# The first unit's V loads, SyncE transfers and hand-written order in a block-sparse attention and feed-forward kernel

## The chip, the cores and the metric

The kernel runs on one core of one Trainium2 chip. The metric is the device time of one execution in microseconds (us). Engines are named as in the profile: PE (TensorE matmuls), PEld (its weight loads), DVE (VectorE), ACT (ScalarE), POOL (GpSimd) and SP (SyncE, which here only issues transfers). Work between engines is ordered by semaphores; each engine runs its own instructions in the order in which the program wrote them.

## The reference

Four batches, eight heads, 768 tokens in 24 blocks of 32, head size 64. Every block of queries sees its own block, the two beside it, the first and the last block, and three sampled blocks; the first and last query block see everything ("dense" rows). The attention output then goes through a feed-forward layer with exact GELU (512 to 2048 to 512).

```
scores = q @ k.T / sqrt(64)                    # per batch and head
mask   = |blk_i - blk_j| <= 1 or blk_i, blk_j in {0, 23} or blk_j in sampled_blocks[blk_i]
attn   = softmax(where(mask, scores, -1e9))
x      = (attn @ v)  as (3072, 512)
out    = gelu_exact(x @ w_in) @ w_out
```

## The kernel before

The work is cut into eight units, two for each batch. Unit 0 of a batch has the query blocks 1 to 11 in three groups of four, four and three (groups 0, 1, 2 of the plan: blocks 4-7, 8-11, 1-3) and the dense rows; unit 1 has blocks 12 to 22. A unit's attention is followed by its feed-forward layer: first `ffn1` products (`hp`, L540), GELU, then `ffn2` products (`op`, L583), which are strewn as fillers into the attention of the next unit. `ffn1` of unit 0 is begun ahead in the attention of unit 0 (`ffn1_ahead`).

The scores of a group of query blocks need, for each block, its keys side by side in the tile `gb`: the first and last block ("fixed", copied by `gather_fixed` with part 1), the three neighbours (part 0), and the three sampled blocks, which `gather` copies one by one, with block numbers held in registers (`block_numbers` loads them from the list `vf`, at line L231, in one register load for up to 22 numbers). In the first unit POOL gathers the sampled keys of groups 1 and 2 (`gather(..., 0, KC, nc.gpsimd)`, 128 columns) and later the sampled values of all three groups (`values_of(t)`, 264 columns, into the tiles `kn` and `g`, which are free then). DVE gathers the sampled keys of group 0. SP copies the fixed blocks of groups 1 and 2: `fixed(1, nc.sync, 1)` gives four transfers, `fixed(2, nc.sync, 1)` two.

V of a batch is loaded by POOL in eight transfers, one for each head, in the order `VORDER` (`load_values`, L149), into `kvs[b % 2]`. Before the lines below, three of the eight have been issued, behind two loads of k (`kn`) and two of q (`qn`):

```
others = block_numbers(grps[1], POOL)      # L674
load_values(0, slice(3, 7))
others |= block_numbers(grps[2], POOL)
load_values(0, slice(7, None))
```

After them POOL gathers the keys of group 1 (6, then 6, with `load_w_in(0)` between), loads the numbers of group 0, issues `load_w_in(1)` and gathers the 9 blocks of keys of group 2. Then `xv0`, `xv1`, `xv2` gather the values of groups 0, 1, 2, with `load_w_in(2)`, `load_w_in(3)` and both halves of `w_out` strewn in, and `xl` loads k and q of batch 1.

The order of everything else in a unit's attention is a plan written out by hand, a string of words. `s0` to `s3` are scores of the four dense rounds, `s4`/`s5`, `s6`/`s7`, `s8`/`s9` of the rounds of groups 0, 1, 2 (two query blocks each, one in s9). `m` is the maximum (DVE), `e` the exponentials (ACT), `t` the turning of the exponentials (DVE). `w` is the product with values for the dense rows (`wd`, in halves `wd0`, `wd1`) or a group (`wa`, `wb`, `wc`: L484), `d` the division (DVE), `o`/`O` the turning of the output (PE, then copied by ACT). `f` with a number issues that many filler products (in unit 0: `idle_products`, L593, whose results nobody uses), 32 in all. `x` with a name calls one of the extra steps: `xp2`, `xp3` turn the q heads of pairs 2 and 3; `xf0`, `xf1`, `xf2` are ACT's copies of neighbours for groups 1 and 2; `xh`, `xi`, `xj` are DVE's for group 0; `xa`, `xb`, `xc` are `ffn1` products ahead; `xn` loads numbers on DVE; `G` loads ACT's table for GELU. Scores go to one of two buffers (`psA`), so that a round of scores waits until the exponentials two rounds earlier are done.

In unit 1, `PLANS[1]` (`xk0d` and so on) turns k and q of batch 1 on PE, at L242, from the tiles that `xl` loads.

Of the kernel before, what the change touches and what calls it, by code (L numbers as in the profile page):

```python
# [11 lines left out]
BF16 = mybir.dt.bfloat16  # L12
# [8 lines left out]
def kernel(  # L21
# [10 lines left out]
    nc = tc.nc  # L32
    P = 128
    B, H, S, D = q.shape
# [9 lines left out]
    VS = 2 * D + 4  # L44
    KC = NPR * BL
# [13 lines left out]
    const = ctx.enter_context(tc.tile_pool(name="const", bufs=1))  # L59
# [11 lines left out]
    kvs = [const.tile([P, NB + 1, BW], BF16, name=f"kv{i}") for i in range(2)]  # L71
# [10 lines left out]
    g = const.tile([P, KOUT, UT], BF16, name="g")  # L82
    mark = const.tile([1, 1], BF16, name="mark")
    junk = const.tile([1, 1], BF16, name="junk")

    HALVES = (slice(0, 4), slice(4, 8))

# [57 lines left out]
    def load_v(b, h):  # L145
        G, hh = divmod(h, 4)
        c0 = KC + VS * G + D * (hh % 2)
        hh ^= G
        nc.gpsimd.dma_start(out=kvs[b % 2][32 * hh:32 * hh + 32, 0:NB, c0:c0 + D],  # L149
                            in_=v[b, h].rearrange("(n p) d -> p n d", p=BL))  # L150


    VORDER = sorted(range(H), key=lambda h: (h // 4, (h % 4 ^ h // 4) % 2, h % 4))

    def load_values(b, at=slice(None)):
        for h in VORDER[at]:
            load_v(b, h)
# [17 lines left out]
    def ones(i):  # L175
        for hh in range(4):
            for G in range(2):
# [6 lines left out]
                      in_=bass.AP(tensor=sb_words, offset=0,  # L184
                                  ap=[[NB * NR * 2, 1], [1, NB * NR * 2]]))
# [40 lines left out]
    def block_numbers(js, engine):  # L226
        flat = vf.rearrange("o j r -> o (j r)")
        vals = []
        for c0 in range(js[0] * NR, (js[-1] + 1) * NR, 22):
            c1 = min(c0 + 22, (js[-1] + 1) * NR)  # L230
            _, got = nc.values_load_multi_w_load_instructions(  # L231
                flat[0:1, c0:c1], engines=[engine], min_val=0, max_val=NB,
                skip_runtime_bounds_check_because="block numbers are below the number of blocks")
            vals += got if isinstance(got, (tuple, list)) else [got]
        return {j: vals[NR * i:NR * i + NR] for i, j in enumerate(js)}
# [46 lines left out]
    def gather_fixed(kT, place, copy=None, part=None, lanes=range(3)):  # L282

        copy = copy or nc.vector.tensor_copy
        groups = gb.rearrange("p (g x) -> p g x", x=GW)
        js = sorted(place)
        runs = [[j for j in js if place[j] - j == c] for c in sorted({place[j] - j for j in js})]
        for run in runs if part != 1 else ():
            i0 = place[run[0]]
            assert i0 % 3 == 0  # L290
            for lane in range(min(3, len(run))):
                if lane not in lanes:
                    continue
                m, g0 = len(range(lane, len(run), 3)), i0 // 3
                c0, j = BW + KC * lane, run[0] + lane - 1
                copy(
                    groups[:, g0:g0 + m, c0:c0 + 3 * BW].rearrange("p g (w c) -> p g w c", c=BW)[:, :, :, 0:KC],
                    kT[:, j:j + 3 * m, :].rearrange("p (g w) c -> p g w c", w=3))
        if part == 0:
            return  # L300
        at = slice(min(place.values()) // 3, max(place.values()) // 3 + 1)
        n = at.stop - at.start
        for to, n0 in ((groups[:, at, 0:3 * KC].rearrange("p g (l c) -> p g l c", c=KC), 0),
                       (groups[:, at, 4 * BW:GW].rearrange("p g (l x) -> p g l x", x=DW)[:, :, :, NR * BW:DW], NB - 1)):
            if copy is nc.sync:
                for x in range(n):
                    nc.sync.dma_start(out=to[:, x], in_=kT[:, n0:n0 + 1, :].to_broadcast([P, 3, KC]))
            else:
                copy(to, kT[:, None, n0:n0 + 1, :].to_broadcast([P, n, 3, KC]))

    def gather(unit, js, at, c0=0, c1=BW, engine=None):

        src = k0 if (unit.b, c1) == (0, KC) else kvs[unit.b % 2][:, :, c0:c1]
        for j in js:
            for r in range(NR):
                to = sampled_values(unit, j, r) if c0 == KC else sampled(unit.place[j], r)[:, c0:c1]
                (engine or nc.vector).tensor_copy(to[:, None, :], src[:, bass.ds(at[j][r], 1), :])  # L317
# [271 lines left out]
    def idle_products(m):  # L589

        op = psO.tile([P, D_MODEL], F32, name="op", tag="op")
        for _ in range(m):
            nc.tensor.matmul(op, lhsT=identity, rhs=qT0[:, 0:2, 0:2, :], start=True, stop=True)  # L593
            yield
# [77 lines left out]
    grps = units[0].groups  # L672
    value_list()
    others = block_numbers(grps[1], POOL)  # L674
    load_values(0, slice(3, 7))
    others |= block_numbers(grps[2], POOL)
    load_values(0, slice(7, None))
    known = block_numbers(grps[0], DVE)
    nc.vector.memset(kvs[1][:, FILLED:NB + 1, KC:BW], 0.0)
    known |= block_numbers(J0[7:9], DVE)  # L680
# [14 lines left out]
    def fixed(t, *how):  # L695
        gather_fixed(k0, {j: units[0].place[j] for j in grps[t]}, *how)
    fixed(1, nc.sync, 1)
    fixed(2, nc.sync, 1)
    gather(units[0], grps[1][:2], others, 0, KC, nc.gpsimd)
    load_w_in(0)  # L700
# [24 lines left out]
    def more_numbers(js):  # L725
        def load():
            for c in range(0, len(js), 6):
                known.update(block_numbers(js[c:c + 6], DVE))
        return load
    attention(units[0], idle_products(32),  # L730
# [3 lines left out]
              {"l": later_keys, "p2": partial(later_pair, 0), "p3": partial(later_pair, 1),  # L734
               "h": lambda: fixed(0, None, 0, (0,)), "i": lambda: fixed(0, None, 0, (1, 2)),
               "j": lambda: fixed(0, None, 1),
# [29 lines left out]
    for n, unit in enumerate(units):  # L766
# [3 lines left out]
        if nxt is not None and not fresh:  # L770
            if n == 0:
                nc.vector.tensor_copy(kvs[0][:, :, 0:KC], k0)
                more_numbers(J1[3:8])()
            gather_fixed(keys(b), nxt.place)
            gather(nxt, J1[:8], known)
            if n == 0:
                more_numbers(J0[:3])()
        for s in range(KOUT // 2):
            ffn1_step(n, 2 * s)
            if s == 0:  # L780
# [4 lines left out]
                elif fresh and b + 2 < B:  # L785
                    xT, t0 = column[b, unit.groups[-2][0]]
# [17 lines left out]
            if fresh and s == 0:  # L804
                gather_fixed(keys(b + 1), nxt.place)
                gather(nxt, J0[3:9], known)
                gather(nxt, J0[:3], known)
                hold_loads(sampled(nxt.place[J0[2]], NR - 1)[0:1, BW - 1:BW])
                gather(nxt, J0[9:], others, engine=nc.gpsimd)
# [43 lines left out]
```

## Time and profile before

| | us |
|---|---|
| median of 3 runs | 274.44 (274.05 to 274.59) |
| profiled execution, its own time | 273.89 |
| its span, first to last instruction | 271.9 |
| PE busy in the span | 255.1 (94%) |
| DVE busy | 203.2 (75%) |
| ACT busy | 207.0 (76%) |
| POOL busy | 103.0 (38%) |

Rows of the timeline give start, duration, engine, line, operation, output tile <- input tiles, how many instructions the row holds, and in brackets the engine's idle time before them and what ended it. "issue" there means that the profile shows nothing that the engine waited for. Rows of the chain give start, duration and what the chain was on. Rows of one line's view give the durations (ns, least/median/most) and the first and last start. Rows of the windows give the stretch, its length, the busy time of PE, PEld, DVE, ACT and POOL with the number of instructions, the granted PE clock, the share of the transfer engines and GB/s.

### The profile page before, as it was taken

The numbers are of one execution on the slowest core, as the hardware profiler recorded it, in microseconds if no ns is written. First come the engines' busy times: TensorE is split into PE (matmuls) and PEld (weight loads), VectorE is DVE, ScalarE is ACT, GpSimd is POOL, SyncE is SP. The second block draws the span as 40 slices with busy tenths as digits, with TensorE's granted clock in tenths as the row PEclk, the third lists the DMA queues.
The fourth block names the chain that finished last, engine by engine and source line by source line (L and its number), as shares of the span: only waits on it lengthen the run. The fifth ranks groups of instructions, "written<-read, shape, count | busy, mean of one in ns | idle before, by whom it ended". The sixth has DMA issues, their size and how long they took to land.

```text
span 271.9 us, 11545 instructions
## 1 busy us (share of the span) xinstructions
PE 255.1 (94%) x4944; PEld 144.8 (53%) x4944; DVE 203.2 (75%) x472; ACT 207.0 (76%) x379; POOL 103.0 (38%) x212
## 2 busy tenths in 40 slices
PE   0789699999999999999999999999999999999995
PEld 0634485455664665545554466455645655465544
DVE  7599758699896989589998987698939993882000
ACT  8789746977868886797868976988788966995611
POOL 7798960735964000950963002920040160000000
PEclk9999979999999999999999999999999999999999
DMA  6999399979999115951999108911101110111012
GB/s 98 185 185 144 66 140 201 206 129 146 95 172 129 41 43 122 122 65 50 104 164 123 60 28 159 112 43 45 40 0 41 46 41 0 41 41 43 0 40 78
DMA packets 75909, 24.40 MB, mean 90 GB/s; under 512 B 65489, under 2 KB 72914, under 8 KB 75858
## 3 DMA queue, kind: packets, MB, share of 16 engines
q0 software_dynamic: 57440, 13.64, 53.7%
q1 hardware_dynamic: 18418, 10.03, 15.5%
q8 instruction: 38, 0.62, 1.0%
q14 instruction: 13, 0.11, 0.1%
HBM read 27.26 MB, written 6.29 MB: 123 GB/s over the span
## 4 chain that ended last, share of the span: by engine, by line
PE 71%; DMA 9%; ACT 7%; POOL 6%; issue 4%; DVE 2%; POOLq 1%; ACTq 0%
PE hp L540 27%; PE op L583 21%; PE av L484 9%; DMA kn<-in_k_dram 6%; PE sc L358 4%; DMA kv<-in_v_dram 3%; ACT L429 2%; PE tx L516 2%; PE op L612 2%; PE av L445 2%; POOL g L317 2%; ACT pp L401 2%; PE pt L242 1%; POOL kv L149 1%; PE av L612 1%
## 5 line engine op out<-in xcount | busy, mean ns | idle before, releaser
L540 PE MATMUL hp<-xT,w_in_sb 128*128 128x384 bf16 (+2 forms) x536 | 85.1, 319 | 0.2 <-issue 0.2
L583 PE MATMUL op<-w_out_sb,g 128*128 128x512 bf16 x336 | 83.9, 380 | 0.4 <-issue 0.4
L401 ACT ACTIVATE pp<-sc,nm 128x256 bf16<-128x256 f32 x176 | 74.4, 546 | 7.5 <-DVE nm L384 7.5
L540 PEld LDWEIGHTS <-w_in_sb 128*128 128x128 bf16 x536 | 51.2, 98 | 33.3 <-issue 0.3
L562 ACT ACTIVATE g<-hp 128x768 bf16<-128x768 f32 x56 | 45.2, 809 | 25.4 <-PE hp L540 25.4
L384 DVE TENSOR_REDUCE nm<-sc 128x4 f32<-128x1024 f32 (+1 forms) x48 | 53.2, 1117 | 10.5 <-PE sc L358 10.2
L583 PEld LDWEIGHTS <-g 128*128 128x128 bf16 x336 | 28.6, 98 | 34.3 <-issue 7.2
L317 DVE COPY gb<-kv 128x392 bf16 x177 | 34.7, 274 | 0.0
L418 DVE STREAM_TRANSPOSE pT<-pp 128x512 f32<-128x512 f32 (+1 forms) x48 | 31.2, 657 | 4.3 <-ACT pp L401 3.8
L317 POOL COPY gb<-kv 128x392 bf16 x54 | 26.3, 537 | 16.1 <-PE av L484 15.7
L173 POOL COPY mark<-gb 1x1 bf16<-1x1 bf16 x6 | 1.1, 178 | 81.3 <-DVE gb L317 81.3
L484 PE MATMUL av<-kv,pT 64*32 64x130 bf16 (+1 forms) x1344 | 28.7, 228 | 1.0 <-DVE pT L418 0.9
L484 PEld LDWEIGHTS <-pT 64*32 64x32 bf16 (+1 forms) x2400 | 26.8, 94 | 5.1 <-DVE pT L418 2.6
L149 POOL DMA_DIRECT2D kv<-in_v_dram x32 | 22.9, 726 | 2.4 <-issue 2.3
L524 ACT COPY xT<-tx 128x512 bf16<-128x512 bf16 (+1 forms) x32 | 13.9, 459 | 11.6 <-PE tx L516 11.3
L358 PE MATMUL sc<-gb,qT 64*32 64x256 bf16 x704 | 18.4, 274 | 2.9 <-issue 1.5
L358 PEld LDWEIGHTS <-qT 64*32 64x32 bf16 x832 | 9.5, 89 | 21.2 <-issue 13.4
L429 ACT ACT_TABLE_LOAD x15 | 19.2, 1283 | 0.2
L387 DVE TENSOR_REDUCE nm<-sc 128x1 f32<-128x768 f32 x16 | 14.7, 947 | 5.9 <-PE sc L358 5.7
L504 DVE TENSOR_TENSOR xh<-av,rec 128x512 bf16<-128x512 f32 (+2 forms) x28 | 18.3, 652 | 1.0
L567 ACT COPY os<-op 128x512 f32<-128x512 f32 (+1 forms) x23 | 13.1, 570 | 6.0 <-PE op L612 4.3
L484 PE MATMUL av<-gb,pT 64*32 64x130 bf16 x924 | 17.2, 222 | 0.0
(80 smaller groups left out, 249.6 us busy)
## 6 DMA issues: line engine op xcount, KB each, us to landing
out_dram<-os SPq DMA_DIRECT2D x23, 256.0 KB, 2.4
kv<-in_v_dram POOLq DMA_DIRECT2D x32, 96.0 KB, 3.7
w_in_sb<-in_moe_w_in_dram POOLq DMA_DIRECT2D x4, 512.0 KB, 7.3
w_out_sb<-in_moe_w_out_dram POOLq DMA_DIRECT2D x2, 1024.0 KB, 13.4
kn<-in_k_dram POOLq DMA_DIRECT2D x4, 384.0 KB, 11.4
qn<-in_q_dram POOLq DMA_DIRECT2D x4, 384.0 KB, 12.8
qn<-in_q_dram POOLq DMA_DIRECT2D x12, 128.0 KB, 4.9
kn<-in_k_dram POOLq DMA_DIRECT2D x12, 128.0 KB, 6.0
```

What stands on the lines that cost most here:

```text
L149: nc.gpsimd.dma_start(out=kvs[b % 2][32 * hh:32 * hh + 32, 0:NB, c0:c0 + D], in_=v[b, h].rearrange("(n p) d -> p n d", p=BL))
L317: (engine or nc.vector).tensor_copy(to[:, None, :], src[:, bass.ds(at[j][r], 1), :])
L358: nc.tensor.matmul(o, lhsT=qT[rows, j // 4, pr, BL * (j % 4):BL * (j % 4) + BL], rhs=rhs(rows, pr), start=True, stop=True)
L384: nc.vector.tensor_reduce(out=nm[:, 0:2 * n].rearrange("p (g j) -> p g j", g=2), in_=A4[:, :, 0:n, :], op=ALU.max, axis=AX.X, negate=True)
L401: nc.scalar.activation(at[:, x // n, x % n], A[:, a:a + 256].rearrange("p (e c k) -> p e c k", e=2, k=BL), AF.Exp, bias=nm[:, x:x + 1])
L418: nc.vector.transpose(pt.rearrange("p g c x -> p (g c) x")[:, :, 64 * s:64 * (s + n)].bitcast(F32), pp[:, 0:512 * n].bitcast(F32).rearrang ...
L429: nc.scalar.activation(junk, zero[0:1, 0:1], func)
L484: nc.tensor.matmul(av[32 * s:32 * (s + w), h, VS * G:VS * G + V2], lhsT=pv[rows, G, c % 4, BL * s:BL * (s + w), c // 4], rhs=src[rows], st ...
L504: nc.vector.tensor_tensor(xh[rows, :, 0:m * D].rearrange("p h (g x d) -> p h g x d", x=2, d=D), a[:, :, :, 0:2 * D].rearrange("p h g (x d) ...
L540: nc.tensor.matmul(hp[:, i, c0:c1], lhsT=w_in_sb[:, ki, (m + i) * P:(m + i + 1) * P], rhs=xTs[n % 2][:, ki, c0:c1], start=(ki == 0), stop= ...
L562: nc.scalar.activation(g[:, m:m + 2, 0:T], hp[:, :, 0:T], AF.Gelu)
L583: nc.tensor.matmul(op, lhsT=g[:, m, t * P:(t + 1) * P], rhs=w_out_sb[:, m, :], start=(m == 0), stop=(m == KOUT - 1))
```

## The change

The eighth V load is issued with the fourth to seventh, ahead of the register load of group 2's block numbers. On SP a small transfer of two elements of the last V head into a new tile `seen` is placed between the four transfers of group 1 and the two of group 2; it reads what the last V load writes, so SP waits there until that load has landed, and group 2's transfers come behind it. The plan of unit 0 is another order of the same words: 32 filler products as before, 23 instead of 28 of them ahead of `s9`; `xf0` and `xh` stand first, `s5` and `m5` ahead of `t3` and `t2`, `xf2` behind `e5`, `G` behind `wb`. In `gather_fixed` the source is named once; the copies are the same.

```
+    seen = const.tile([1, 2], BF16, name="seen")
...
-    load_values(0, slice(3, 7))
+    load_values(0, slice(3, None))
     others |= block_numbers(grps[2], POOL)
-    load_values(0, slice(7, None))
     known = block_numbers(grps[0], DVE)
...
     fixed(1, nc.sync, 1)
+
+    hh, c0 = VORDER[-1] % 4 ^ VORDER[-1] // 4, KC + VS * (VORDER[-1] // 4) + D * (VORDER[-1] % 2)
+    nc.sync.dma_start(out=seen, in_=kvs[0][32 * hh:32 * hh + 1, 0, c0:c0 + 2])
     fixed(2, nc.sync, 1)
...
-              "xj xp2 xv0 s0 xp3 s1 m0 f1 xv1 f1 e0 xi m1 e1 xh s2 f1 s3 t0 xf0 m2 e2 f1 m3 t1 e3 f2 s4 xf1 f8 m4 "
-              "e4 t3 t2 s5 f1 xf2 wd0 s6 f1 xv2 wd1 f2 m5 f2 e5 t4 m6 f2 dd s7 t5 e6 m7 od f2 s8 t6 wa xl e7 f4 "
-              "m8 s9 da e8 m9 t7 t8 e9 t9 f2 oa wb wc db ob dc xn xa Oc xb f2 G xc",
+              "xf0 xj xh xp2 s0 xp3 m0 xv0 s1 f1 e0 xi s2 m1 e1 f1 s3 f1 t0 f1 m2 e2 m3 t1 e3 f3 s4 xv1 f1 m4 s5 "
+              "m5 t3 f1 xf1 t2 f3 xv2 e4 e5 f3 s6 wd0 wd1 f2 t4 xf2 m6 s7 dd t5 e6 f3 m7 e7 f2 s8 od t6 wa xl m8 "
+              "e8 da f1 s9 m9 t7 f4 e9 t8 t9 f3 oa wb G db wc ob dc xn f1 xa Oc xb f1 xc",
```

More of the change, by code (lines that the diff above doesn't have):

```diff
@@ L304, in gather_fixed @@
                        (groups[:, at, 4 * BW:GW].rearrange("p g (l x) -> p g l x", x=DW)[:, :, :, NR * BW:DW], NB - 1)):
+            fixed_block = kT[:, None, n0:n0 + 1, :].to_broadcast([P, n, 3, KC])
             if copy is nc.sync:
                 for x in range(n):
-                    nc.sync.dma_start(out=to[:, x], in_=kT[:, n0:n0 + 1, :].to_broadcast([P, 3, KC]))
+                    nc.sync.dma_start(out=to[:, x], in_=fixed_block[:, x])
             else:
-                copy(to, kT[:, None, n0:n0 + 1, :].to_broadcast([P, n, 3, KC]))
+                copy(to, fixed_block)
     def gather(unit, js, at, c0=0, c1=BW, engine=None):
```

## The prediction

> **What bounds the kernel now.** I read the page first, then the chain that ended last in order of time, then the timeline of each engine over the first 55 us, since the change touches nothing later.
>
> ```profile
> span 271.9 us, 11545 instructions
> PE 255.1 (94%) x4944; PEld 144.8 (53%) x4944; DVE 203.2 (75%) x472; ACT 207.0 (76%) x379; POOL 103.0 (38%) x212
> ```
>
> TensorE (PE) is busy for 94% of the span, so time is lost or won only where PE waits. The chain shows where the first unit is tied to something else than PE:
>
> ```profile
> 10.82 0.71 POOLq L231
> 11.53 1.44 issue
> 12.99 7.93 DMA kv<-in_v_dram
> ...
> 33.55 0.69 POOL w_in_sb L162
> 34.24 1.73 POOL w_out_sb L167 x2
> 35.97 16.87 DMA kn<-in_k_dram
> ```
>
> The reader is to see that for the first 53 us the chain is not on PE. It goes through GpSimd (POOL): reading block numbers, the eighth V load, that load's flight, a row of gathers, three weight loads, the load of batch 1's keys (kn). Those keys land at 35.97 + 16.87 = 52.84 and PE turns them at 52.88. How far PE is from being the bound itself at that point:
>
> ```profile
> 52.88 0.53 PE L242 MATMUL pt<-identity,kn 96*64 96x96 bf16 x16 [0.47 <-DMA kn<-in_k_dram]
> ```
>
> PE waits 0.47 us for kn. So two paths meet at 52.88: the POOL path, and PE's own work, which is 0.47 us shorter. From there PE runs on almost without a gap. Whichever path is later after the change sets the new time. A gain of PE alone in the first unit is worth nothing, and a gain of POOL alone at most 0.47 us; a loss of POOL counts in full.
>
> **The POOL path, step by step.**
>
> ```profile
> 8.70 2.83 POOL L149 DMA_DIRECT2D kv<-in_v_dram  x4 [0.25 <-issue]
> 12.99 0.71 POOL L149 DMA_DIRECT2D kv<-in_v_dram  x1 [1.46 <-issue]
> 13.75 1.47 POOL L317 COPY gb<-qT 128x128 bf16 x6
> ...
> 18.24 2.17 POOL L317 COPY gb<-qT 128x128 bf16 x9
> 21.24 3.20 POOL L317 COPY kn<-kv 128x264 bf16 x9 [0.84 <-DMA kv<-in_v_dram]
> ...
> 26.16 7.38 POOL L317 COPY g<-kv 128x264 bf16 x21
> 33.50 0.74 POOL L162 DMA_DIRECT2D w_in_sb<-in_moe_w_in_dram  x1
> 34.23 1.77 POOL L167 DMA_DIRECT2D w_out_sb<-in_moe_w_out_dram  x2
> 35.97 0.71 POOL L118 DMA_DIRECT2D kn<-in_k_dram  x1
> ```
>
> Seven V loads are out by 11.53. Then come the third group's nine block numbers, the eighth V load at 12.99, and the key gathers, which run without a gap from 13.75 to 18.24 + 2.17 = 20.41. POOL then stands 0.84 us until V has landed (12.99 + 7.93 = 20.92; the first value gather is at 21.24). From 21.24 to the issue of kn at 35.97 it has no hole: every shift at 21.24 reaches kn. So the most that an earlier V can give here is the hole of 0.84 us, and only if the key gathers don't move.
>
> They do move. The change puts the eighth V load ahead of the nine numbers, and both are in POOL's instruction order ahead of the first key gather. What the numbers cost, from the rows of the register loads (by the code: nine values from element 3 of the list in the first row, twelve from 24, twelve from 12, nine from 60, and on VectorE (DVE) fifteen from 45 and nine from 3):
>
> ```profile
> L231 POOLq TENSOR_LOAD <-vf x1: 2273/2273/2273, 10.2 to 10.2; - x1
> L231 POOLq TENSOR_LOAD <-vf x1: 1025/1025/1025, 7.1 to 7.1; - x1
> L231 POOLq TENSOR_LOAD <-vf x1: 1236/1236/1236, 15.0 to 15.0; - x1
> L231 POOLq TENSOR_LOAD <-vf x1: 827/827/827, 32.4 to 32.4; - x1
> L231 DVEq TENSOR_LOAD <-vf x1: 3410/3410/3410, 38.1 to 38.1; - x1
> L231 DVEq TENSOR_LOAD <-vf x1: 2061/2061/2061, 47.5 to 47.5; - x1
> ```
>
> The lists that begin at an element divisible by 4 cost 0.83 to 1.24 us, the others (3, 45, 3) 0.23 to 0.25 us a value. The third group begins at 3, so it costs 2.27 us and not about 1. In the kernel before, this read begins at 10.2 while POOL is still busy issuing V loads six and seven: of its 2.27 us, 1.3 lie beside that work. After the change it can begin only when the eighth V load has been handed out, and that load has a wait of its own: the view of the second q load lists it among those that waited for its landing (the load that comes eight places earlier in POOL's row of loads). The first row below is that entry, the others show when PE saw the two q loads.
>
> ```profile
>   POOL kv L149: 1.5, 1
> 9.95 0.85 PE L242 MATMUL pq<-identity,qn 96*64 96x96 bf16 x16 [0.37 <-DMA qn<-in_q_dram]
> 12.02 0.85 PE L242 MATMUL pt<-identity,qn 96*64 96x96 bf16 x16 [0.57 <-DMA qn<-in_q_dram]
> ```
>
> The first q load has landed just before 9.95 and the second just before 12.02. The seventh V load waits in the same way for the first, and the register load behind it began at 10.2: 0.2 to 0.3 us after that landing. So I put the eighth V load at 12.0 (1.0 us earlier than now), and the register load at 12.2, done at 12.2 + 2.27 = 14.5. Now: done at 12.44, and the next instruction on the engine at 12.99, which is 0.55 us for moving the numbers; with 0.15 us for the gather's own address the first key gather comes 0.7 us behind, at 15.2 instead of 13.75: 1.4 us later. The key gathers then end at 20.41 + 1.4 = 21.8. V is down by then: it was down at 20.92, is issued 1.0 us earlier, and two SyncE transfers no longer run beside it. The 0.84 us hole is gone, and the value gathers begin at 21.8 instead of 21.24: 0.6 us later. What was hidden (1.3 us of register load beside V loads) now stands open, and it is more than the hole that it closes.
>
> Bounds of this term: a register load of 0.83 us, the cheapest row, would start the key gathers at 12.2 + 0.83 + 0.7 = 13.7, as now; V, some 0.5 us earlier at 20.4, plus the 0.3 us that the first gather took behind the landing, starts the value gathers at 20.7: -0.5 us. A register load of 2.5 us gives +0.85. I take +0.6, since the same nine numbers from the same place cost 2.27 and 2.06.
>
> [...]
>
> The kn load then goes out at 36.6 and, the queue ahead of it (the same three weight loads) being shifted with it, lands at 53.4; PE turns it at 53.5: +0.6 us.
>
> **SyncE's transfers.** Before, six of them are issued from 10.55 on; four remain, and the last two follow a two-element read that waits for V.
>
> ```profile
> 10.55 6.00 SPq L307 DMA_DIRECT2D gb<-qT  x6
> DMA to landing us min/median/max: 7.3/7.6/9.6
> ```
>
> Nothing else stands in SyncE's queue until the first output. The two are issued at about 20.8 and 21.5. In the crowd of V loads such a transfer took 7.3 to 9.6 us; here only weight loads run beside it, so I take about 4 to 5 us, landing at 25 to 26.5, with 31.1 as the far end. Who waits: the scores of the third group (s8, s9).
>
> ```profile
> 27.08 0.41 PE L358 MATMUL sc<-gb,qT 64*32 64x256 bf16 x16 [0.35 <-ACT pp L401]
> ...
> 31.33 0.29 PE L358 MATMUL sc<-gb,qT 64*32 64x256 bf16 x4 [1.47 <-issue]
> 31.56 0.60 PE L593 MATMUL op<-qT,identity 128*128 128x512 bf16 x2
> ```
>
> s8 is at 27.08 and, by the new order, again near 27 (it still needs the exponentials two rounds back). Cost taken: nothing, with up to 4 us at the far end.
>
> **The new order.** ScalarE's (ACT's) window copies xf0 move ahead of the turned q heads into idle time; xf2 moves behind e5, which lets e5 run earlier; DVE does m5 before t3 and t2, so the dense values wd start about 1 us later, while the second half of wd now follows the first directly. I estimate these to cancel by s8. After s9, seven filler products instead of two stand before the second group's values (wb), and the table load G moves to where ACT is idle; ACT is not what PE waits for there. PE's clock:
>
> ```profile
> 29.95:33.36 3.41, 1.37 (x18) 0.74 (x17) 1.88 (x4) 1.86 (x6) 3.41 (x11) 1.00 0.02 5
> 33.36:36.78 3.42, 3.42 (x195) 3.21 (x192) 1.73 (x6) 0.47 (x2) 3.42 (x6) 0.50 0.53 55
> ```
>
> PE was busy for 1.37 of 3.41 us, and in the next 3.42 us its granted clock (the third figure from the end) was 0.50. More fillers before wb may keep the clock up, worth 3.42 x 0.5, at most 1.7 us; or they only push wb back by five products (0.60 / 2 each: at most 1.5 us). PE thus comes to kn between 1.7 us earlier and 1.5 us later. It may be 0.47 + 0.6 = 1.1 us later before it costs anything. I take zero: kn covers the whole reordering, either way.
>
> The sum: 0 (PE side, covered) + 0.6 (kn later) = +0.6 us on the profiled execution's 273.89, which lies 0.55 below the median of the runs, 274.44. On the median: 275.0, +0.2%.
>
> **Rivals.**
> *The register load is no hindrance* (the other sign): it costs about 1 us behind the V load, or runs ahead of the wait, the key gathers stay at 13.75, and V's earlier landing counts. For it: three of four POOL loads cost 0.83 to 1.24. Against it: the start at element 3. The price is worked out above: value gathers at 20.7, kn 0.5 us earlier, 273.9 if PE keeps up, 274.4 if PE is half a microsecond later itself. It decides where the first key gather starts at 14.3 or earlier (then key gathers end before 21.0 and POOL gains).
> *PE becomes the late path*: SyncE's two transfers land after 27.5 and hold s8, and with it od, wa and s9 in PE's order; or PE, now waiting over 1 us for kn, has its clock halved once more (up to 1.7 us). For it: the 7.3 to 9.6 us row. Against it: 1.1 us of cover. It gives +0.9 to +2 us: 275.3 to 276.4. [...]
> *The change moves V no earlier*: the landing may be set by the packets in flight, not by the issue at 12.99. By the forecast that does not matter, because the key gathers end later than V lands; it stays +0.6.
>
> **How the numbers follow.** Forecast (with the third rival, same time): 0.53. Register load no hindrance: 0.25. PE late: 0.22. A measurement of this kernel can tell about 0.2% (0.55 us) from no change. The forecast's own spread, +0.4 to +0.85, straddles that: 0.27 of its 0.53 count as slower, 0.26 as same. Of the second case, 0.12 faster and 0.13 same; all of the third is slower. Together 0.12 faster, 0.39 same, 0.49 slower. The range is 274.0 to 276.3: it takes in most of the cases on both sides and leaves out the ends of the second (below 274.0) and of the third (above 276.3). The likeliest case's own range is 274.8 to 275.3.
>
> **What would show it.** Right: the eighth V load near 12.0 and a register load of over 2 us behind it; first key gather at 15 or later; no wait for V ahead of the first value gather, which starts at 21.6 to 22; kn landing at 53.2 to 53.6 with PE waiting for it longer than 0.47 us. Wrong: a first key gather by 14.3; PE waiting in s8 for SyncE's transfer; or kn landing with PE not waiting for it, which would mean that the reordering itself set the time.

## The result: 0.5% slower, more than was forecast

| | before | after |
|---|---|---|
| median (19 runs each) | 274.66 us | 275.79 us |
| ratio after to before | | 1.005, 95% interval 1.0027 to 1.0073 |
| profiled execution, span | 271.9 us | 274.6 us |

The medians differ by 1.13 us, the ratio stands for 1.4 us (0.7 to 2.0). The two profiled executions differ by 2.7 us in span. That is more than the change: the one of before took 273.89 us (0.8 under its median), the one of after 276.71 (0.9 over its). In the one of after PE's products also ran slower for longer at the start (the third dense round of scores took 0.83 us, and 0.51 in the one of before); it took 0.83 us in every profile of the new order below and 0.81 us or more in three of the eight of the old one, so this goes mostly with the order. Times of PE are read with care below, and the runs in many rounds decide. GpSimd's times in the first 25 us are firmer: kernels below whose instructions are the same up to there have them within 0.2 us. Three executions that ran much longer than the others of their kernel, one each in three of the experiments, are left out of the ratios.

### The profile page after: what moved, and what is told of

Same layout as the page of the kernel before. It is cut to its first block, busy times and chain, and to the rows that moved or that the text cites. A ratio compares the mean times of both kernels' runs of the same rounds, so it can differ in the third digit from the quotient of the medians.

```text
span 274.6 us, 11547 instructions
## 1 busy us (share of the span) xinstructions
PE 254.9 (93%) x4944; PEld 143.5 (52%) x4944; DVE 203.5 (74%) x472; ACT 207.0 (75%) x379; POOL 103.0 (37%) x212
## 4 chain that ended last, share of the span: by engine, by line
PE 81%; ACT 8%; DVE 4%; issue 3%; DMA 3%; POOL 1%; POOLq 0%; ACTq 0%
PE hp L542 30%; PE op L585 22%; PE av L486 10%; PE sc L360 6%; DMA qn<-in_q_dram 3%; PE tx L518 3%; ACT L431 2%; ACT pp L403 2%; PE av L447 2%; PE op L614 2%; DVE nm L386 2%; PE pt L243 2%; PE op L595 2%; ACT pp L407 1%; PE av L614 1%
## 5 line engine op out<-in xcount | busy, mean ns | idle before, releaser
L486 PE MATMUL av<-kv,pT 64*32 64x130 bf16 (+1 forms) x1344 | 27.5, 221 | 1.7 <-issue 1.4
L486 PEld LDWEIGHTS <-pT 64*32 64x32 bf16 (+1 forms) x2400 | 25.5, 91 | 6.7 <-issue 2.4
L407 ACT ACTIVATE pp<-sc,nm 128x768 bf16<-128x768 f32 x16 | 16.8, 1102 | 1.6 <-DVE nm L389 1.5
```

The costliest lines, as they stand in the source:

```text
L407: nc.scalar.activation(pp[:, 0:S].rearrange("p (c k e) -> p c e k", e=2, k=BL), A[:, 0:S].rearrange("p (c e k) -> p c e k", e=2, k=BL), AF ...
L486: nc.tensor.matmul(av[32 * s:32 * (s + w), h, VS * G:VS * G + V2], lhsT=pv[rows, G, c % 4, BL * s:BL * (s + w), c // 4], rhs=src[rows], st ...
```

## The profile after

The timeline of GpSimd (POOL), from the eighth V load to the load of batch 1's keys:

```profile
12.34 0.76 POOL L150 DMA_DIRECT2D kv<-in_v_dram  x1 [0.78 <-DMA qn<-in_q_dram]
16.44 1.47 POOL L319 COPY gb<-qT 128x128 bf16 x6 [3.34 <-DVE nm L389]
...
20.76 2.17 POOL L319 COPY gb<-qT 128x128 bf16 x9
22.88 3.19 POOL L319 COPY kn<-kv 128x264 bf16 x9
...
27.80 7.38 POOL L319 COPY g<-kv 128x264 bf16 x21
35.14 0.74 POOL L163 DMA_DIRECT2D w_in_sb<-in_moe_w_in_dram  x1
35.87 1.77 POOL L168 DMA_DIRECT2D w_out_sb<-in_moe_w_out_dram  x2
37.62 0.71 POOL L119 DMA_DIRECT2D kn<-in_k_dram  x1
```

The eighth V load goes out at 12.34 instead of 12.99, held by the second q load as forecast. Behind it POOL stands 3.34 us before its first key gather, at 16.44 instead of 13.75. (The row names a DVE instruction, a maximum. In the kernel before the same gather started at 13.75 while the first of these, from 13.68 to 14.64, was still running, so it needs none of them; the register load fills 12.3 to 16.13.) The hole of 0.84 us before the value gathers is gone, but they begin at 22.88 instead of 21.24. From there everything is shifted as it stands: w_in, w_out and kn are asked for 1.64 to 1.65 us later. The register loads of the third group and of group 0, and the flight of kn:

```profile
L232 POOLq TENSOR_LOAD <-vf x1: 3825/3825/3825, 12.3 to 12.3; - x1
L232 POOLq TENSOR_LOAD <-vf x1: 810/810/810, 18.2 to 18.2; - x1
DMA to landing us min/median/max: 17.1/17.1/17.1
```

The nine numbers took 3.83 us, not 2.27. kn lands at 37.62 + 17.1 = 54.7, 1.9 us later than before (54.72 against 52.84). SyncE's (SP's) two transfers behind the wait, and PE at the points that the prediction names:

```profile
21.34 1.32 SPq L309 DMA_DIRECT2D gb<-qT  x2
DMA to landing us min/median/max: 6.6/6.8/6.9
```

```profile
28.77 0.71 PE L360 MATMUL sc<-gb,qT 64*32 64x256 bf16 x16 [1.17 <-DVE pT L420]
33.09 1.04 PE L595 MATMUL op<-qT,identity 128*128 128x512 bf16 x4 [0.81 <-issue]
37.19 0.27 PE L486 MATMUL av<-kv,pT 64*32 64x130 bf16 x7 [1.42 <-issue]
...
52.77 2.98 PE L585 MATMUL op<-w_out_sb,g 128*128 128x512 bf16 x13
55.68 0.53 PE L243 MATMUL pt<-identity,kn 96*64 96x96 bf16 x16
```

The two transfers land near 28.3 and 28.6, and s8 starts at 28.77, right behind the second: the scores of the third group did wait for them here. (The row names a DVE instruction that ends at 28.76; in the profile of the changed kernel with twelve numbers, below, s8 starts at 28.09 while the same DVE instruction is still running, so s8 does not need it.) PE reaches the turn of kn at 55.68 with no wait: in this execution kn had been there for about 1 us, and PE's own path was the later one.

## The experiments

Ratios are to the kernel before, measured beside it in the same rounds; brackets hold the 95% interval. Three theories stood at the start: A, the register load that now stands open behind the V load; B, the new order makes PE late by itself; C, SyncE's late transfers hold s8.

### The V load first, alone

```
-    load_values(0, slice(3, 7))
+    load_values(0, slice(3, None))
     others |= block_numbers(grps[2], POOL)
-    load_values(0, slice(7, None))
```

> The kernel before with one part of the change alone: the eighth V load ahead of the third group's register load; old order, no wait on SyncE. Theory A (the loss is on GpSimd: the register load now stands open behind the V load): register load 3.5 to 3.9 us, first key gather at 16.2 to 16.6, first value gather at 22.6 to 23.0, kn landing at 54.2 to 54.8 with PE waiting for it; time +1.0 to +1.6 us against the kernel before. Theory B (the new order makes PE late, by itself): the GpSimd times move, but the time stays within 0.4 us of the kernel before, or is at most that of kn. Theory C (SyncE's late transfers hold s8): no change in s8, time within 0.4 us.

Measured: 1.0057 [1.0028, 1.0085], as much as the whole change. The register load, the first key gather and the first value gather:

```profile
L231 POOLq TENSOR_LOAD <-vf x1: 4357/4357/4357, 12.1 to 12.1; - x1
16.77 1.48 POOL L317 COPY gb<-qT 128x128 bf16 x6 [3.92 <-DVE gb L296]
23.25 3.21 POOL L317 COPY kn<-kv 128x264 bf16 x9
33.59 0.40 PE L358 MATMUL sc<-gb,qT 64*32 64x256 bf16 x4 [3.15 <-issue]
```

The load took 4.36 us, 0.5 us past what A gave, and the gathers start 0.2 to 0.3 us past it; kn's landing, near 54.7, is inside. The forecast sign "PE waiting for kn" did not show in this profile either: PE turned kn at 56.25. The last row is s9. Behind that hole PE's granted clock was 0.51 from 32.7 to 39.6, and the mean granted clock was 0.994 or less in all twelve executions of this kernel; it was 0.998 or more in 18 of 34 of the kernel before beside it and in 14 of the 19 of the changed kernel. So the two losses are alike in size but probably not made up alike: here PE at a clock of 0.51 is likely to have a part.

### The new order alone

The plan string of the changed kernel, V and SP as before.

> The kernel before with the new order of the first unit's plan alone; V and SyncE as before. A: kn still lands at 52.8 and covers the reordering: within 0.4 us of the kernel before. B: +0.8 to +1.4 us, PE reaching the turn of kn after it has landed, with no wait for it. C: within 0.4 us.

Measured: 0.999 [0.9952, 1.0027]. B falls: the order costs nothing that can be measured. But its profile looks like B, which is a warning about single profiles:

```profile
L118 POOL DMA_DIRECT2D kn<-in_k_dram x1: 712/712/712, 35.7 to 35.7; - x1
DMA to landing us min/median/max: 16.7/16.7/16.7
42.58 9.48 PE L540 MATMUL hp<-xT,w_in_sb 128*128 128x384 bf16 x47 [2.19 <-issue]
55.46 0.53 PE L242 MATMUL pt<-identity,kn 96*64 96x96 bf16 x16
```

kn lands at 52.4, PE comes at 55.46, 2.6 us later than in the profile of before; yet over all the runs the time is the same. In this execution the clock was halved for a stretch behind the hole (0.52 from 43.65 to 47.05), which makes the 47 products take 9.48 us; in the profile of the changed kernel they take 7.80.

### The changed kernel with the V load put back

```
-    load_values(0, slice(3, None))
+    load_values(0, slice(3, 7))
     others |= block_numbers(grps[2], POOL)
+    load_values(0, slice(7, None))
```

> The changed kernel with the eighth V load put back behind the register load; SyncE's wait and the new order stay. A: register load 2.2 to 2.4 us, first key gather at 13.7 to 13.9, kn at 52.7 to 53.0, time within 0.4 us of the kernel before (0.8 to 1.5 us under the changed one). B and C: +0.8 to +1.4 us, as the changed kernel, with PE late at kn (B) or s8 waiting for SyncE's transfers until 28.5 or later (C).

Measured: 0.9983 [0.995, 1.0016]:

```profile
L232 POOLq TENSOR_LOAD <-vf x1: 2427/2427/2427, 10.3 to 10.3; - x1
14.00 1.48 POOL L319 COPY gb<-qT 128x128 bf16 x6
20.89 3.22 POOL L319 COPY kn<-kv 128x264 bf16 x9 [0.37 <-DMA kv<-in_v_dram]
```

kn landed at 52.2. The loss is gone with this one line, although the new order and the wait on SP remain. B and C both fall as its cause. (PE came to kn at 55.45 in this profile too, 3.2 us after it had landed, and the median of the runs is still not above that of the kernel before.)

### The wait on SP alone

> The kernel before with SyncE's wait for V alone (the two-element read ahead of group 2's two transfers). A (all of the loss is the register load behind the V load): within 0.4 us of the kernel before; V lands 0.2 to 0.5 us earlier, group 2's transfers at 25 to 27, s8 not held. C (late transfers hold s8): +0.4 to +1.2 us, s8 after 28.

Measured: 0.9979 [0.996, 0.9999]. The last V load landed near 20.1 (0.8 us earlier than before, with two fewer transfers beside it), so the value gathers followed the key gathers at once:

```profile
20.46 3.21 POOL L318 COPY kn<-kv 128x264 bf16 x9
```

That is 0.78 us earlier than before. Group 2's transfers landed at 25.7 and 26.0, ahead of s8 at 27.25. This part of the change is, if anything, a gain of 0.2%.

### The same changes with the register load made cheaper

```
-    others |= block_numbers(grps[2], POOL)
+    others |= block_numbers([0] + grps[2], POOL)
```

In the changed kernel:

> The changed kernel, but the third group's register load takes twelve numbers from element 0 (block 0's too, which nobody uses) instead of nine from element 3. A with the price by the list's start: load 1.0 to 1.6 us, first key gather at 14.0 to 14.6, first value gather at 20.8 to 21.3, kn at 52.4 to 53.0, time within 0.4 us of the kernel before. A with the price by the V packets in flight at that time (not by the start): load 3.5 us or more, time +1.0 us or more. B: GpSimd's times fall but the time stays +0.8 to +1.4 us.

Measured: 0.9958 [0.9928, 0.9989]. In the kernel before:

> The kernel before, but the third group's register load takes twelve numbers from element 0 instead of nine from element 3. If the list's start sets the price: load about 1.0 to 1.2 us (from 10.2), eighth V load at 12.0 to 12.2 (held by the second q load), first key gather at 12.7 to 13.0, key gathers end near 19.5, value gathers start behind V at 20.7 to 21.0, time 0 to -0.5 us. If the traffic sets it: load 2.2 us or more, all as before, time unchanged.

Measured: 1.0003 [0.9979, 1.0027]. In the kernel with the V load first alone:

> The kernel before with the eighth V load first and the twelve numbers from element 0 behind it; old order, no wait on SyncE. A: load 2.0 to 2.3 us in the V traffic, first key gather at 14.5 to 14.8, value gathers at 21.0 to 21.3, time within 0.4 us of the kernel before, 1.0 to 1.8 us under the same kernel with nine numbers from element 3. B and C say nothing of this pair.

Measured: 1.0012 [0.9992, 1.0032], against 1.0057 with nine numbers from element 3. The register loads of the three, in this order, and their first key and value gathers:

```profile
L232 POOLq TENSOR_LOAD <-vf x1: 2147/2147/2147, 12.3 to 12.3; - x1
14.70 1.48 POOL L319 COPY gb<-qT 128x128 bf16 x6 [1.61 <-DVE nm L389]
21.18 3.21 POOL L319 COPY kn<-kv 128x264 bf16 x9
```

```profile
L231 POOLq TENSOR_LOAD <-vf x1: 811/811/811, 10.3 to 10.3; - x1
13.13 1.48 POOL L317 COPY gb<-qT 128x128 bf16 x6
20.97 3.22 POOL L317 COPY kn<-kv 128x264 bf16 x9 [1.17 <-DMA kv<-in_v_dram]
```

```profile
L231 POOLq TENSOR_LOAD <-vf x1: 2296/2296/2296, 12.3 to 12.3; - x1
14.88 1.48 POOL L317 COPY gb<-qT 128x128 bf16 x6 [1.78 <-DVE nm L387]
21.35 3.21 POOL L317 COPY kn<-kv 128x264 bf16 x9
```

With the load 1.7 to 2.1 us cheaper the loss is gone, in the changed kernel and in the one with the V load alone: the register load is the cause. (In the changed kernel the two intervals lie apart; in the pair with the V load alone they just overlap, 1.0028 and 1.0032.) Both prices that were weighed against each other hold at once. From the same place in the program, twelve numbers from element 0 cost a third of nine from element 3 (0.81 us against 2.09 to 2.43 in the six kernels that read them near 10.3), and either list costs 1.3 to 2.3 us more when it is read behind the eighth V load (2.15 and 2.30; 3.76 to 4.36). In the kernel before, the cheaper load gains nothing at the end: the key gathers come 0.6 us earlier, and POOL then waits 1.17 us for V instead of 0.84.

### Which path carries the delay to the end

POOL's delay makes two things late, the value gathers and the loads behind them. First, kn ahead of w_out in the changed kernel:

```
             load_kq(kn, k, hs, 1)
+            if hs is HALVES[0]:
+                load_w_out(0, 2)
+                load_w_out(1, 2)
             load_kq(qn, q, hs, 1)
```

> The changed kernel, with the first half of batch 1's keys loaded ahead of the two w_out loads (w_out then lands about 2 us later). If the path to the end is kn's landing: kn lands near 45, the time falls by 0.8 to 1.6 us against the changed kernel, to that of the kernel before. If it is the late value gathers, which hold the products with values on PE: kn lands near 45 too, but the time stays +0.8 to +1.6 us over the kernel before.

Measured: 1.0053 [1.0026, 1.0079]. It does not decide, since the edit itself asks for w_out 0.55 us later (36.42 instead of 35.87), and PE now waits for that:

```profile
53.85 1.24 PE L585 MATMUL op<-w_out_sb,g 128*128 128x512 bf16 x5 [1.16 <-DMA w_out_sb<-in_moe_w_out_dram]
55.02 0.53 PE L243 MATMUL pt<-identity,kn 96*64 96x96 bf16 x16
```

kn landed at 43.3, but PE now waits 1.16 us for the second half of w_out. The prediction had named kn alone; w_out stands right beside it. The profile settles something else. Up to 35 us this is the program of the changed kernel, with POOL as late (value gathers at 22.76), and yet SP's two transfers were faster:

```profile
21.31 1.32 SPq L309 DMA_DIRECT2D gb<-qT  x2
DMA to landing us min/median/max: 4.8/5.0/5.2
28.56 0.58 PE L360 MATMUL sc<-gb,qT 64*32 64x256 bf16 x16 [0.47 <-ACT pp L403]
```

They landed by 27.2 at the latest, and s8 did not wait for them. So the late landing in the changed kernel's profile does not follow from POOL's delay alone; it can differ from one execution to the next.

For the path to the end, the whole row of loads has to be delayed or not. In the kernel before, five copies that nobody uses, at one of two places:

```
             gather(units[0], js[:3], others, KC, BW, nc.gpsimd)
+            if t == 2:                  # the other kernel: t == 0, ahead of the gather
+                for _ in range(5):
+                    nc.gpsimd.tensor_copy(pad, kvs[0][:, 0, KC:BW])
```

> The kernel before with five copies that nobody uses (about 0.35 us each, 1.75 us in all) on GpSimd behind the last value gather, ahead of the last w_in load: w_in, w_out and batch 1's k and q are asked for 1.75 us later, the value gathers are on time. If the loads are the path that sets the end (as the prediction had it): kn lands at 54.4 to 54.7, PE waits for it, time +1.1 to +1.5 us, much as with the eighth V load first. If late value gathers are what costs: within 0.4 us of the kernel before.

> The kernel before with the same five copies ahead of the first value gather: value gathers and loads are both 1.75 us later (first gather at 22.8 to 23.1), key gathers on time. If the loads are the path: the same time as with the copies behind the gathers, +1.1 to +1.5 us. If late value gathers are what costs: +1.0 to +1.8 us here, and clearly more than with the copies behind them.

Measured: loads alone late 1.0085 [1.0049, 1.0121], more than was expected; gathers and loads late 1.0049 [1.0016, 1.0082]. The dose was 2.27 us, not 1.75 (0.45 us a copy). POOL and PE with the loads alone late, and PE's clock around the wait:

```profile
33.38 2.27 POOL L714 COPY pad<-kv 128x264 bf16<-128x264 bf16 x5
35.59 0.74 POOL L163 DMA_DIRECT2D w_in_sb<-in_moe_w_in_dram  x1
53.50 1.44 PE L584 MATMUL op<-w_out_sb,g 128*128 128x512 bf16 x5 [2.35 <-DMA w_out_sb<-in_moe_w_out_dram]
55.37 0.85 PE L243 MATMUL pt<-identity,kn 96*64 96x96 bf16 x16 [0.43 <-DMA kn<-in_k_dram]
50.90:54.40 3.50, 1.15 (x7) 0.39 (x4) 1.25 (x2) 3.27 (x8) 3.37 (x14) 1.00 1.24 206
54.40:61.20 6.80, 6.37 (x73) 2.33 (x72) 3.63 (x5) 1.39 (x3) 0.08 (x1) 0.50 0.98 185
```

and with both late:

```profile
23.72 3.20 POOL L318 COPY kn<-kv 128x264 bf16 x9
35.98 0.74 POOL L163 DMA_DIRECT2D w_in_sb<-in_moe_w_in_dram  x1
52.54 1.24 PE L584 MATMUL op<-w_out_sb,g 128*128 128x512 bf16 x5 [1.32 <-DMA w_out_sb<-in_moe_w_out_dram]
54.46 0.53 PE L243 MATMUL pt<-identity,kn 96*64 96x96 bf16 x16 [0.69 <-DMA kn<-in_k_dram]
```

Late loads cost the time by themselves, with the value gathers on time; making the gathers late too adds nothing. PE waits first for w_out, then for kn. In the first of the two the wait of 2.35 us for w_out was also followed by half the clock for 6.8 us, which the second, with waits of 1.32 and 0.69 us, was spared. The runs bear this out: the mean granted clock was 0.998 or more in 2 of 12 executions with the loads alone late, in 7 of 12 with both late and in 14 of 35 of the kernel before beside them. Among these alone the medians are 276.3 (of two), 275.8 and 274.0 us, so late loads cost about 2 us at full clock too; the two delayed kernels are not told apart.

### The register load hidden

The numbers of group 2 read behind the key gathers of group 1, all V first, with SP's wait; in the new order and in the old.

```
-    others |= block_numbers(grps[2], POOL)
...
     gather(units[0], grps[1][2:], others, 0, KC, nc.gpsimd)
+    others |= block_numbers([0] + grps[2], POOL)
     others |= block_numbers(grps[0], POOL)
```

> The changed kernel with the third group's numbers (twelve from element 0) read behind group 1's key gathers instead of ahead of them: the register load then lies beside gathers that are already queued. First key gather at 12.8 to 13.4, no hole of more than 0.8 us behind it, value gathers as soon as V is down, 20.5 to 21.0, kn at 51.8 to 52.6. Register load as the cause: -0.5 to -1.5 us against the kernel before, at or under the one with twelve numbers read ahead. Order or SyncE as the cause: above the kernel before.

> The kernel before with SyncE's wait, all eight V loads first and the third group's numbers read behind group 1's key gathers; old order. Same GpSimd times as the changed kernel with late numbers. If the new order is worth something: 0.3 to 0.8 us slower than that one; if not: the same, -0.5 to -1.0 us against the kernel before.

Measured: new order 0.9975 [0.9937, 1.0014], old order 0.9973 [0.9942, 1.0004]. POOL in the new order:

```profile
L232 POOLq TENSOR_LOAD <-vf x1: 1202/1202/1202, 14.5 to 14.5; - x1
13.16 1.61 POOL L319 COPY gb<-qT 128x128 bf16 x6
20.72 3.21 POOL L319 COPY kn<-kv 128x264 bf16 x9 [0.73 <-PE sc L360]
```

The register load (14.5 to 15.7) lies beside gathers and a weight load that keep POOL busy from 13.16 to 16.95, and the key gathers start right behind the V load (12.36 + 0.76 = 13.12). The ratio is about 0.75% under the changed kernel's and the same in both orders. Against the kernel before, the changed kernel with the register load cheap, the two with it hidden and SP's wait alone stand between 0.996 and 0.998. Of these only the changed kernel with twelve numbers (0.9958) and SP's wait alone (0.9979) have intervals below 1; the experiments don't rank them. The two without SP's wait but with twelve numbers (1.0003 and 1.0012) gain nothing.

## Why the prediction was right, and where it was off

**The path** was right on POOL. The loss enters between the eighth V load and the first key gather and comes through the value gathers without a hole to the row of loads. One line of the change carries it (1.0057 alone, 0.9983 without it), and in the kernel before, late loads alone cost as much or more, at a somewhat larger dose (2.27 us). That it reaches PE as late weights and keys in the changed kernel too is likely but not shown: its profile has PE at kn with no wait, and so has the one with the V load alone. Two of the prediction's own signs of being wrong did show in that one profile, the wait in s8 and kn landing with PE not waiting. The second was to mean that the reordering set the time; the order alone (0.999) and the V load alone in the old order (1.0057) say that it did not.

**The time**, 275.79 us, is outside the likeliest case's own range (274.8 to 275.3) and inside that of the rival in which PE becomes late (275.3 to 276.4). The wide range holds it because it made room for that rival; the mechanism is the forecast one with a larger term.

**The term of the sum that was mis-sized is the register load: 3.83 us instead of 2.27.** With it the first key gather was at 16.44, not 15.2, the value gathers 1.64 us later, not 0.6, and kn at 54.7, not 53.4. The 0.7 us that the prediction set between the end of the load and the gather were 0.3 (12.3 + 3.83 = 16.13, gather at 16.44), which hid part of the miss. Of their two parts, the 0.55 us is the gap from 12.44 to 12.99 in the profile of before; that moving the numbers took it was an estimate, and no run shows the 0.15 us for the gather's address by itself. The bound that I gave it, 2.5 us, was too tight: the rows for such a list were read under less traffic (on POOL from 10.2; the share of the transfer engines was 1.79 from 10.20 to 12.40, and 2.26 from 12.30 to 16.10 in the profile after) or without V in flight (on DVE at 47.5, 2.06 us). The row that I took was right for the same nine numbers, but not for the place to which the change moves them. That the traffic is what makes the load longer there was not shown by itself; no run read the list at 12.3 without V in flight.

**The price at the end** was about 1.1 to 1.4 us for kn's shift of 1.9 us, though the interval (0.7 to 2.0) takes in 1.9. The sum took the 0.47 us of PE's slack from one profiled execution. In other profiles PE comes to kn about 3 us after it has landed, even with POOL on time (the new order alone, the V load put back), so kn is not the last to arrive in every execution, and a late kn is then covered in part. Which of the two paths ends last in the median run of the changed kernel stays open; its one profile shows PE. There PE is level with the kernel with twelve numbers at s7 (26.00 and 26.01), 0.7 us behind it at s8 (28.77 and 28.09) and 1.5 us behind where the 47 `ffn1` products start (44.48 and 42.96); what lies between are holes that the profile puts down to nothing.

**"kn covers the whole reordering"**: right as to the time (0.999 for the order alone), but the reason is not shown: PE did not wait for kn in the profile after, and came 3 us after it in that of the order alone. The clock that more fillers were to keep up was kept up in the profile after (PE busy for 2.60 us from 29.95 to 33.36, and 1.00 instead of 0.50 in the next 3.42 us); no gain in time came of it. **w_out** was left out of that step; its second half landed at 51.0 in the profile of before (35.1 + 15.9), amid the products with w_out, which run from 49.44 to 52.42, and it is the first to be waited for when the loads are late.

**SP's transfers**: I put their landing at 25 to 26.5 and their cost at nothing. They landed near 28.3 and 28.6, and s8 did follow them. With POOL on time they landed at 25.7 to 26.0; with POOL as late, in the kernel with kn asked for early, by 27.2, and s8 did not wait. So the flight of 6.6 to 6.9 us belongs to the one execution at least in part, and what made it long was not found. The rival's share of the loss was not measured by itself; it is not needed for a loss (the V load alone has no such wait), and SP's wait alone gains.

**The rival of a cheap register load** was the right counter-case: with 2.15 us instead of 3.83 the changed kernel ends under the one before.

**The half clock**, which one rival put behind a longer wait for kn, came with the loads late: 0.50 from 54.40 to 61.20, behind a wait of 2.35 us for w_out and a stretch of 3.50 us in which PE was busy for 1.15. The run with gathers and loads late had 1.55 of the same 3.50 us busy and kept 1.00. What decides between the two was not shown.

## What to carry to other kernels

Before moving a transfer ahead of a register load, ask what the register load was hidden behind: here 1.3 of its 2.27 us lay beside V loads, and in POOL's one order the move took them out into the open (3.34 us with POOL standing), behind a transfer with a wait of its own (0.78 us for the second q load). Price a moved instruction for the conditions at its new place, not by its row at the old one, and widen the bound where no row has those conditions. When a row of loads is issued just in time, look at all of them for the first to be waited for, not only at the one that the chain names; and decide by repeated times: executions of the changed kernel alone ran from 274.87 to 278.11 us, more than twice the effect.

## What the runs showed of the hardware that was not expected

In these runs a register load of block numbers on POOL cost by where its list starts and by when it is read: twelve numbers from element 0 took 0.81 us near 10.3, 1.20 at 14.5 and 2.15 to 2.30 behind the eighth V load; nine from element 3 took 2.09 to 2.43 and 3.76 to 4.36. Here the fewer numbers cost more. Nine numbers from element 60 took 0.83 us in the kernel before, so it is not their count alone.

PE has holes of 0.8 to 2.2 us in the changed kernel, and one of 3.15 us with the V load alone, that the profile puts down to nothing ("issue"), and they move with the order of instructions. Ahead of and in the one of 2.19 us before 44.48 of the changed kernel, the transfer queue that the profile calls "instruction" moved no packet from 37.3 to 42.2 and one from 42.2 to 44.5. Whether the hole has to do with that queue, no run here shows.
